# Gated mix of linear and softmax attention, one core: products of kv with the output weights in 16 tiles of 32x32, returned through DRAM

## The chip, the cores and the metric

The kernel runs on one core of a Trainium2 chip. The metric is the device time of one execution in microseconds, and the kernel before has a median of three runs. The engines are named as in the profile: PE is TensorE (PEld its weight loads), DVE is VectorE, ACT is ScalarE, POOL is GpSimd, SP is SyncE, which issues all DMAs here.

## The reference

Two attention blocks over the same x (1 x 2048 x 1024, fp32, 32 heads of 32) are mixed by a gate per token. B is softmax attention. A is linear attention: its kv is one 32x32 matrix a head, and its output goes through `wo`.

```python
x = A_x
g = _sigmoid((x * gate_w).sum(-1, keepdims=True))
# A: q, k, v = x @ wqkv, 32 heads
phi = lambda t: jnp.where(t > 0, t + 1, jnp.exp(t)) + 1e-6
pq, pk = phi(q), phi(k)
kv = einsum("bhsd,bhse->bhde", pk, v)
z = einsum("bhsd->bhd", pk)
num = einsum("bhqd,bhde->bhqe", pq, kv)
den = einsum("bhqd,bhd->bhq", pq, z)[..., None] + 1e-6
a = merge_heads(num / den) @ A_wo
# B
p = softmax(einsum("bhqd,bhkd->bhqk", q, k) * Dh ** -0.5)
b = merge_heads(einsum("bhqk,bhkd->bhqd", p, v)) @ B_wo
return g * a + (1 - g) * b
```

Since kv is the same for all tokens, the kernel does not form `num`: it multiplies each head's kv into that head's 32 rows of `A_wo` once, and the turned queries pq / den then go through the product.

## The kernel before, in words

All products of x and of the outputs with weights are fp32 in three products of a high and a low part (`three`, L148 to L150: high x high, high x low, low x high, each 128x128 by 512 columns). A part comes from a cast on ACT and a subtraction on DVE or POOL (`split`, L254 and L255). The main stage is one stream of PE instructions, made of several that a planner interleaves:

- `heads_`: for each of 32 heads, 64 score products (L902), each followed by an exponential on ACT (L906); in three groups of 5, 5 and 6 key blocks a head, the products with v (L994). A block is four products, each on a tile of 128x32 of the array, all into bank 4. The sums over keys are added on POOL (L951) and, for the last 512 columns, on DVE (L960). `finish` (L805) sums over partitions at the end of a head, just ahead of a group of the next head, and four reciprocals (L812) and a multiplication (L815) on DVE follow.
- `maxima`: the same 64 scores a head, transposed, two heads ahead (L752), each reduced on DVE (L757); `rows` (L762, L768) turns the maxima into two extra rows of the queries.
- `linear`: the chunks "v", "kv" (four), "q" (two) and "o" (two), each with 16 tiles of tokens and eight blocks k of the contraction. x tiles come from DRAM by `load_xp` (L479), two units ahead, for "o" the turned queries `oA_d`. Chunk "kv" accumulates kv of its eight heads in `keys` (L505, added on DVE in L514); "q" computes phi, divides (L660 to L674), and `queries` turns the tiles (L566) and stores them (L573); "o" writes its result to `ra_d` (L687, L688).

While the last token tile of a chunk runs, `split_w` replaces the eight weight blocks for the next chunk one by one, each block k after its last use. For "o" it is a product: the raw `a_wo` block (loaded by `load_w`, L262) is multiplied by `kvb`, a tile with the kv of four heads on the diagonal of 128x128 and zeros elsewhere (memset L635, copies L518), and the result is cast (L457) and subtracted (L458) into the weight tile:

```python
b = take()
end = lin_pe(4.0, free[b])
nc.tensor.matmul(pb, kvb[:, k, :], raw, start=True, stop=True)       # L455
```

That is sixteen products, eight ahead of each of the two "o" chunks; both operands are plain fp32, which runs as two passes.

Order: the instruction order on every engine is written out by the planner (`tc.manual_schedule`). It keeps an estimated end time for each engine (`T`, `use`), hands out the six PSUM banks of `RING` (`take`, `give`), defers DVE's work (`defer`, `fill`) and always advances the stream that is furthest behind its goal. The linear stream's pace in "kv" and "o" is

```python
cost = {"kv": NT * (D // HC) * (pace + 1) + 2 * (D // HC), "q": NQC * NT * (pace + 2),
        "o": NQC * (NT * pace + 4 * NK)}
rates["kv"] = rates["o"] = (cost["kv"] + cost["o"] - RESERVE) / (steps - cost["q"] / RATE_Q)
```

with pace 24, 2048 steps, RATE_Q 2.6 and RESERVE 56. After the last head, `output` multiplies B's output with `B_wo` and adds the two.

Of the kernel before, what the change touches and what calls it, by code (L numbers as in the profile page):

```python
# [45 lines left out]
def kernel(  # L46
# [32 lines left out]
    def f32(ap):  # L79
        return ap.bitcast(F32)  # L80
# [9 lines left out]

    xs = [[dram.tile([P, NK, P], F32, name=f"xs{p}_{t}") for t in range(NT)] for p in range(2)]
# [4 lines left out]
    v_d = [dram.tile([P, NT, C], F32, name=f"v{c}") for c in range(NQC)]  # L96
    ra_d = [dram.tile([P, D], F32, name=f"ra{t}") for t in range(NT)]
# [7 lines left out]
    kvb = sb.tile([P, NK, P], F32, name="kvb")  # L105
# [260 lines left out]
    kv_flat = kvb.rearrange("p k c -> p (k c)")  # L366

    def gate():
        for t in range(NT):
            for i in range(2):  # L370
                xn, junk = kv_flat[:, :HD], kv_flat[:, HD:]
# [62 lines left out]

    def load_w(kind, c, k, n):
        if kind == "v":
            raw = load_cols(b_wqkv, vcols(c), k, n)
        elif kind == "kv":
            raw = load_cols(a_wqkv, [(D + c * HC, HC), (2 * D + c * HC, HC)], k, n)
        else:  # L440
            raw = load_cols(a_wqkv if kind == "q" else a_wo, [(c * C, C)], k, n)
        return raw, T["pe"] + 4.0

    def split_w(kind, c, k, raw, at, eng):

        hi, lo = wpart(k, 0), wpart(k, 1)
        w_left[k].clear()
        if kind == "o":
            yield from keys_alone(len(units))
            need(k_left)  # L450
            yield lambda: both(bank_at(), at)
            b = take()
            pb = bank[b]
            end = lin_pe(4.0, free[b])
            nc.tensor.matmul(pb, kvb[:, k, :], raw, start=True, stop=True)  # L455
            end = use("act", 0.5, end)
            nc.scalar.copy(hi, pb)  # L457
            item = defer(lambda _: nc.vector.tensor_sub(lo, pb, f32(hi)), end)  # L458
# [32 lines left out]
    kv_acc = mid[8][:, :NK * DH].rearrange("p (k d) -> p k d", d=DH)  # L491

    def keys(n, c, t, pk, va, todo):
# [3 lines left out]
        def products(b, at):  # L497
# [9 lines left out]
            acc = kv_acc[:, c * GC:(c + 1) * GC, :]  # L507

            def total(_):
                part = pb.rearrange("p (k d) -> p k d", d=DH)  # L510
                if t == 0:
                    nc.vector.tensor_copy(acc, part)
                else:
                    nc.vector.tensor_add(acc, part, acc)  # L514
                if t == NT - 1:
                    for r in range(4):
                        rows = slice(r * DH, (r + 1) * DH)
                        nc.gpsimd.tensor_copy(kvb[rows, c * GC:(c + 1) * GC, rows], acc[rows])  # L518
# [16 lines left out]
    def keys_alone(n):  # L535

        while kv_todo and kv_todo[0][0] <= n:
            yield lambda: both(kv_todo[0][1](), bank_at()) if kv_todo else 0.0
            if kv_todo and kv_todo[0][0] <= n:
                use("pe", AV_SWITCH, kv_todo[0][1]())  # L540
                keys_now(T["pe"])

# [37 lines left out]
    def linear():  # L580
# [4 lines left out]
        for n, (i, t) in enumerate(units):  # L585
# [14 lines left out]
            for k in range(NK):  # L600
# [15 lines left out]
                if k == NK - 1:  # L616
                    yield from extra
                if follow and t == NT - 2 and k < min(LEAD_W, NK):
                    coming_w.append(load_w(*follow, k, LEAD_W + 1))
                if follow and t == NT - 1:  # L620
                    yield from split_w(*follow, k, *coming_w.popleft(), nc.vector if kind == "v" else nc.gpsimd)
# [9 lines left out]
            elif kind == "kv":  # L631
                va = mid[7][:, (n % 2) * HC:(n % 2 + 1) * HC]
                yield from keys_alone(n - 2)
                if c == t == 0:
                    nc.gpsimd.memset(kvb, 0.0)  # L635
# [48 lines left out]
            else:  # L684
                res = mid[8 + n % 2]
# [182 lines left out]
    def heads_():  # L868
# [3 lines left out]
        raws[2:6] = [spare[:, i * C:(i + 1) * C] for i in range(4)]  # L872
        o_ring.append(spare)
# [57 lines left out]
    def attend(h, lacc):  # L931
# [50 lines left out]
        def av(t0, t1):  # L982
# [95 lines left out]
    def output():  # L1078
# [30 lines left out]
        for n in range(NT):  # L1109
# [12 lines left out]
            "o": NQC * (NT * pace + 4 * NK)}  # L1122
# [111 lines left out]
```

## Time and profile before

| | |
|---|---|
| median of 3 runs | 2903.78 us (2903.44 to 2906.72) |
| the profiled execution | 2902.3 us |
| its span, first to last instruction | 2900.5 us |
| granted TensorE clock, mean | 0.999 |
| DMA moved, mean rate | 364.88 MB, 126 GB/s |

How to read the rows: a group has the line, the engine, the operation, output <- inputs with partitions x elements, then the count, busy microseconds, the mean nanoseconds of one, and the engine's idle time ahead of them with what ended it. "128*32" behind a matmul is rows * columns of the array that it uses. In a timeline the first number is the start in microseconds from the start of the span, the second the duration from the first to the last end of the merged instructions; matmuls are pipelined, so one that lasts 0.39 us may follow another after 0.23. In a row of windows stand the stretch, its length, busy time and count of PE, PEld, DVE, ACT and POOL, the granted clock, the busy share of the DMA engines and GB/s.

### The profile page before, as it was taken

What the parts mean: (1) busy time and instruction counts of PE and PEld (TensorE: products, weight loads), DVE (VectorE), ACT (ScalarE), POOL (GpSimd) and SP (SyncE); (2) the same over time, 40 slices, a digit from 0 to 9 for tenths busy, and PEclk for the clock granted to TensorE, in tenths of its full rate; (3) what the DMA queues carried; (4) which work ended last, traced back from release to release, by engine and by line L of the source; (5) the groups of instructions that cost most, each with busy time, mean ns of one, the idle gap of its engine ahead of it and who ended that gap; (6) DMA issues with size and microseconds to landing.
All of it is one profiled execution on the core that took longest, in us unless ns stands there. A gap on an engine that the chain in (4) does not pass through costs nothing.

```text
span 2900.5 us, 43785 instructions
## 1 busy us (share of the span) xinstructions
PE 2888.7 (100%) x15840; PEld 2076.8 (72%) x15840; DVE 2057.6 (71%) x3451; ACT 1522.4 (52%) x2840; POOL 1775.7 (61%) x599
## 2 busy tenths in 40 slices
PE   9999999999999999999999999999999999999999
PEld 8888888766666666767667667676666666666787
DVE  3222114888888888888888888888887888886622
ACT  4111111466666667666766666666566666666410
POOL 0000001388898889888898896787769887786000
PEclk9999999999999999999999999999999999999999
DMA  6687333322343224222333334545443334323542
GB/s 196 211 268 236 120 124 102 115 88 89 90 125 98 90 89 119 93 88 91 117 90 95 100 117 139 157 151 160 138 151 104 105 107 130 100 88 120 197 154 78
DMA packets 273309, 364.88 MB, mean 126 GB/s; under 512 B 91146, under 2 KB 167434, under 8 KB 269962
## 3 DMA queue, kind: packets, MB, share of 16 engines
q1 hardware_dynamic: 273092, 362.07, 40.6%
q8 instruction: 125, 2.05, 0.3%
q14 instruction: 92, 0.75, 0.1%
HBM read 260.31 MB, written 100.40 MB: 124 GB/s over the span
## 4 chain that ended last, share of the span: by engine, by line
PE 97%; POOL 1%; DMA 1%; DVE 1%; issue 0%; ACT 0%; SPq 0%; POOLq 0%; ACTq 0%
PE bank L902 16%; PE bank L148 16%; PE bank L150 16%; PE bank L149 16%; PE bank L752 16%; PE bank L994 15%; PE bank L805 1%; POOL big L951 1%; PE bank L566 1%; PE bank L505 0%; DVE mx L757 0%; PE bank L455 0%; DMA mid<-in_a_wqkv 0%; POOL big L465 0%; DMA mid<-in_xT 0%
## 5 line engine op out<-in xcount | busy, mean ns | idle before, releaser
L951 POOL TENSOR_TENSOR big<-big,big 128x1536 f32<-128x1536 f32 (+1 forms) x434 | 1556.7, 3587 | 188.0 <-ACT big L906 165.5
L757 DVE TENSOR_REDUCE mx<-bank 128x1 f32<-128x512 f32 x2048 | 1312.9, 681 | 318.4 <-PE bank L752 314.5
L906 ACT ACTIVATE big<-bank 128x512 f32<-128x512 f32 x2048 | 1181.5, 601 | 525.6 <-PE bank L902 455.9
L902 PE MATMUL bank<-big,big 128*128 128x512 f32 x2048 | 811.6, 398 | 1.1 <-DMA big<-ml 0.5
L752 PE MATMUL bank<-big,big 128*128 128x512 f32 x2048 | 807.9, 395 | 3.8 <-ACT big L906 2.5
L148 PE MATMUL bank<-big,big 128*128 128x512 f32 x2048 | 801.3, 391 | 1.5 <-ACT big L254 1.4
L150 PE MATMUL bank<-big,big 128*128 128x512 f32 x2048 | 799.2, 390 | 0.0
L149 PE MATMUL bank<-big,big 128*128 128x512 f32 x2048 | 799.1, 390 | 0.0
L902 PEld LDWEIGHTS bank<-big,big 128*128 128x128 f32 x2048 | 384.0, 188 | 164.5 <-issue 67.8
L994 PE MATMUL bank<-big,mid 128*32 128x512 f32 x4096 | 458.5, 593 | 0.0
L752 PEld LDWEIGHTS bank<-big,big 128*128 128x128 f32 x2048 | 384.8, 188 | 93.4 <-ACT big L906 6.2
L148 PEld LDWEIGHTS bank<-big,big 128*128 128x128 f32 x2048 | 384.8, 188 | 87.8 <-DVE mx L757 3.0
L149 PEld LDWEIGHTS bank<-big,big 128*128 128x128 f32 x2048 | 384.8, 188 | 80.1 <-issue 0.8
L150 PEld LDWEIGHTS bank<-big,big 128*128 128x128 f32 x2048 | 384.8, 188 | 79.7 <-DVE big L255 0.6
L707 POOL MEMSET big<- 32x2048 f32 x3 | 5.4, 1808 | 530.7 <-PE bank L149 459.6
L994 PEld LDWEIGHTS bank<-big,mid 128*32 128x32 f32 x4096 | 129.0, 110 | 262.4 <-issue 262.4
L960 DVE TENSOR_TENSOR bank<-bank,big 128x512 f32<-128x512 f32 (+1 forms) x434 | 280.8, 647 | 10.0 <-ACT big L906 8.0
L255 DVE TENSOR_TENSOR mid<-bank,mid 128x512 fp32r<-128x512 f32 x64 | 44.3, 692 | 264.6 <-ACT mid L254 264.6
L947 POOL TENSOR_TENSOR big<-big,big 128x1536 f32<-128x1536 f32 (+1 forms) x31 | 111.6, 3599 | 139.8 <-ACT big L906 139.8
L254 ACT CAST mid<-bank 128x512 fp32r<-128x512 f32 x64 | 37.6, 587 | 291.6 <-PE bank L150 262.5
L812 DVE RECIPROCAL bank<-bank 128x128 f32<-128x128 f32 x128 | 123.3, 963 | 3.3 <-PE bank L805 0.3
L255 DVE TENSOR_TENSOR big<-mid,big 128x512 fp32r<-128x512 f32 x96 | 64.2, 687 | 74.7 <-ACT big L254 74.5
(76 smaller groups left out, 998.0 us busy)
## 6 DMA issues: line engine op xcount, KB each, us to landing
big<-xs SPq DMA_DIRECT2D x192, 512.0 KB, 4.1
qk<-mid SPq DMA_DIRECT2D x128, 256.0 KB, 2.8
big<-oA SPq DMA_DIRECT2D x64, 512.0 KB, 4.1
big<-qk SPq DMA_DIRECT2D x96, 256.0 KB, 4.5
big<-qk SPq DMA_DIRECT2D x384, 64.0 KB, 2.0
xs<-big SPq DMA_DIRECT2D x64, 256.0 KB, 4.2
oA<-mid SPq DMA_DIRECT2D x64, 256.0 KB, 2.8
mid<-in_b_wqkv SPq DMA_DIRECT2D x48, 256.0 KB, 3.9
```

Of the source, the lines that this page charges most:

```text
L148: yield nc.tensor.matmul(ps, sh, mh_, start=(kt == 0), stop=False)
L149: yield nc.tensor.matmul(ps, sh, ml_, start=False, stop=False)
L150: yield nc.tensor.matmul(ps, sl, mh_, start=False, stop=(kt == NK - 1))
L752: nc.tensor.matmul(bank[b], q[:, t * P:(t + 1) * P], k[:, j * C:(j + 1) * C], start=True, stop=True)
L757: nc.vector.tensor_reduce(m[:, t, j:j + 1], bank[b], AX.X, ALU.max)
L812: nc.vector.reciprocal(pl[:, sl], pl[:, sl])
L902: nc.tensor.matmul(bank[b], k[:, t * P:(t + 1) * P], q[:, j * C:(j + 1) * C], start=True, stop=True)
L906: nc.scalar.activation(pr_t[i][:, j * C:(j + 1) * C], bank[b], AF.Exp, scale=SCALE)
L947: nc.gpsimd.tensor_add(lacc[:, :qp], pr(0)[:, :qp], pr(1)[:, :qp])
L951: nc.gpsimd.tensor_add(lacc[:, :qp], lacc[:, :qp], pr(t)[:, :qp])
L960: nc.vector.tensor_add(lacc[:, qp:] if t == NT - 1 else l_b[:, :n], l_b[:, :n], src)
L994: nc.tensor.matmul(av_b[j * DH:(j + 1) * DH, :], v[:, t, :], pr(t)[:, j * C:(j + 1) * C], start=(t == 0), stop=(t == NT - 1))
```

## The change

The products of kv with `a_wo` leave the change of weights. They are now done in four groups `mix()`, one for each half of the contraction (four blocks k) and each "o" chunk, each inside a group of products with v: sixteen products of 32 rows by 32 columns by 512, each head's kv with its own 32 rows of `a_wo`, on sixteen tiles of the array, into four banks of the ring (one a row group). `kvb` shrinks to the kv as accumulated (128 x 8 x 32), so the memset, the diagonal copies and the separate accumulator go. Each bank is cast on ACT and subtracted on DVE as before, and both parts are stored to DRAM (`wa_d`). At the last tile of the chunk before, `load_wa` loads the finished parts straight into the weight tiles. The raw `a_wo` blocks are loaded at tiles 2 and 8 of the first "q" chunk and of the first "o" chunk; tile 14 of these waits, in the planner, until the group is placed. A group is placed where the planner finds four of the six banks free, after at least two blocks of the group with v. The gate's scratch moves from `kvb` to a big tile, and the results of "o" use other tiles for their stores. The planner's cost of "o" loses its 4 NK a chunk.

```diff
-    kvb = sb.tile([P, NK, P], F32, name="kvb")
+    kvb = sb.tile([P, NK, DH], F32, name="kvb")
...
+    def load_wa(c, k):
+        for p in range(2):
+            nc.sync.dma_start(f32(wpart(k, p)), wa_d[p][k // HK][c][k % HK])
+        w_ready[k] = T["pe"] + 5.0
...
     def split_w(kind, c, k, raw, at, eng):
         hi, lo = wpart(k, 0), wpart(k, 1)
-        w_left[k].clear()
-        if kind == "o":
-            yield from keys_alone(len(units))
-            need(k_left)
-            yield lambda: both(bank_at(), at)
-            b = take()
-            pb = bank[b]
-            end = lin_pe(4.0, free[b])
-            nc.tensor.matmul(pb, kvb[:, k, :], raw, start=True, stop=True)
-            end = use("act", 0.5, end)
-            nc.scalar.copy(hi, pb)
-            item = defer(lambda _: nc.vector.tensor_sub(lo, pb, f32(hi)), end)
-            give(b, 0.0, [item])
-            w_left[k].append(item)
-            return
...
-                if t == NT - 1:
-                    for r in range(4):
-                        rows = slice(r * DH, (r + 1) * DH)
-                        nc.gpsimd.tensor_copy(kvb[rows, c * GC:(c + 1) * GC, rows], acc[rows])
...
+    mix_todo = deque((a, c) for c in range(NQC) for a in range(NK // HK))
+    mix_hi, mix_lo = [], (mid[7], mid[10], mid[0], mid[1])
+
+    def load_mix():
+        a, c = mix_todo.popleft()
+        for i in range(HK):
+            nc.sync.dma_start(mix_hi[i], a_wo[(a * HK + i) * P:(a * HK + i + 1) * P, c * C:(c + 1) * C])
+        mix_here.append((a, c, T["pe"] + 8.0))
+
+    def mix_ready():
+        times = [ended(readers[b], free[b]) for b in RING if not held[b]]
+        return (mix_here and not kv_todo and ended(k_left, mix_here[0][2]) is not None
+                and ended(k_left, mix_here[0][2]) <= T["pe"]
+                and sum(at is not None and at <= T["pe"] for at in times) >= 4)
+
+    def mix():
+        a, c, _ = mix_here.pop()
+        need(k_left)
+        bs = [take() for _ in range(4)]
+        end = use("pe", AV + 0.2)
+        for r in range(4):
+            rows = slice(r * DH, (r + 1) * DH)
+            for i in range(HK):
+                nc.tensor.matmul(bank[bs[r]][i * DH:(i + 1) * DH, :], kvb[rows, a * HK + i, :],
+                                 mix_hi[i][rows, :], start=True, stop=True)
+        for r in range(4):
+            hi, lo, pb = f32r(mix_hi[r]), f32r(mix_lo[r]), bank[bs[r]]
+            at = use("act", 0.5, end)
+            nc.scalar.copy(hi, pb)
+
+            def low(_, r=r, hi=hi, lo=lo, pb=pb):
+                nc.vector.tensor_sub(lo, pb, f32(hi))
+                for p, src in enumerate((hi, lo)):
+                    nc.sync.dma_start(wa_d[p][a][c][:, r * DH:(r + 1) * DH, :], f32(src))
+                mixed.append((a, c))
+
+            give(bs[r], 0.0, [defer(low, at)])
...
+            if kind in ("q", "o") and c == 0 and t in (2, 8, NT - 2):
+                yield lambda: None if mix_here else 0.0
+                if t < NT - 2:
+                    load_mix()
...
+                if follow and follow[0] == "o":
+                    if t == NT - 1:
+                        w_left[k].clear()
+                        yield lambda: 0.0 if mixed.count((k // HK, follow[1])) == 4 else None
+                        load_wa(follow[1], k)
+                    continue
...
-                res = mid[8 + n % 2]
+                res = mid[(7, 10)[n % 2]]
...
+        mix_hi.extend(raws[2:6])
...
-            end = use("pe", AV * len(blocks_))
             for t in blocks_:
+                if mix_here:
+                    fill(T["pe"])
+                    if t - t0 > 1 and mix_ready():
+                        mix()
+                end = use("pe", AV)
                 for j in range(NJ):
                     nc.tensor.matmul(av_b[j * DH:(j + 1) * DH, :], v[:, t, :], pr(t)[:, j * C:(j + 1) * C],
                                      start=(t == 0), stop=(t == NT - 1))
...
-            "o": NQC * (NT * pace + 4 * NK)}
+            "o": NQC * NT * pace}
```

More of the change, by code (lines that the diff above doesn't have):

```diff
@@ L96 @@
     v_d = [dram.tile([P, NT, C], F32, name=f"v{c}") for c in range(NQC)]
+    wa_d = [[[dram.tile([HK, P, C], F32, name=f"wa{p}_{a}_{c}") for c in range(NQC)] for a in range(NK // HK)]
+            for p in range(2)]
     ra_d = [dram.tile([P, D], F32, name=f"ra{t}") for t in range(NT)]
@@ L365 @@
     nc.sync.dma_start(zrep, bass.AP(tensor=gate_w.tensor, offset=gate_w.offset, ap=[[0, P], [1, D]]))
-    kv_flat = kvb.rearrange("p k c -> p (k c)")
+    gate_t = f32(big[LACC[1]])
     def gate():
@@ L440, in load_w @@
         else:
-            raw = load_cols(a_wqkv if kind == "q" else a_wo, [(c * C, C)], k, n)
+            raw = load_cols(a_wqkv, [(c * C, C)], k, n)
         return raw, T["pe"] + 4.0
@@ L490 @@
     kv_todo = deque()
-    kv_acc = mid[8][:, :NK * DH].rearrange("p (k d) -> p k d", d=DH)
     def keys(n, c, t, pk, va, todo):
@@ L506, in products @@
                                      start=True, stop=True)
-            acc = kv_acc[:, c * GC:(c + 1) * GC, :]
+            acc = kvb[:, c * GC:(c + 1) * GC, :]
             def total(_):
@@ L541, in keys_alone @@
                 keys_now(T["pe"])
+    mix_todo = deque((a, c) for c in range(NQC) for a in range(NK // HK))
+    mix_here = []
+    mixed = []
+    mix_hi, mix_lo = [], (mid[7], mid[10], mid[0], mid[1])
[17 more added lines that the diff above has]
+            for i in range(HK):
+                nc.tensor.matmul(bank[bs[r]][i * DH:(i + 1) * DH, :], kvb[rows, a * HK + i, :], mix_hi[i][rows, :],
+                                 start=True, stop=True)
+        for r in range(4):
[8 more added lines that the diff above has]
+            give(bs[r], 0.0, [defer(low, at)])
     z_end = [0.0, 0.0]
@@ L620, in linear @@
                 if follow and t == NT - 1:
-                    yield from split_w(*follow, k, *coming_w.popleft(), nc.vector if kind == "v" else nc.gpsimd)
+                    split_w(*follow, k, *coming_w.popleft(), nc.vector if kind == "v" else nc.gpsimd)
                     if k + LEAD_W < NK:
@@ L633, in linear @@
                 yield from keys_alone(n - 2)
-                if c == t == 0:
-                    nc.gpsimd.memset(kvb, 0.0)
                 nc.scalar.copy(va, ps[:, HC:])
```

2 lines of the change are left out of this document (1 added, 1 removed).

## The prediction

> **What bounds the kernel now.** I read the page first: busy times, chain.
>
> ```profile
> span 2900.5 us, 43785 instructions
> ...
> PE 2888.7 (100%) x15840; PEld 2076.8 (72%) x15840; DVE 2057.6 (71%) x3451; ACT 1522.4 (52%) x2840; POOL 1775.7 (61%) x599
> ...
> PE 97%; POOL 1%; DMA 1%; DVE 1%; issue 0%; ACT 0%; SPq 0%; POOLq 0%; ACTq 0%
> ```
>
> PE lies on 97% of the chain and is idle for 2900.5 - 2888.7 = 11.8 us in all. So the time is PE's work plus few waits: a microsecond of array time taken out is a microsecond of the kernel, unless a wait takes its place. Then the list of PE's waits, longest first (its first row), and the groups by shape that the change touches or leans on.
>
> ```profile
> PE bank L752 <- ACT big L906: 2.5, 2, 2.2
> ```
>
> ```profile
> L455 PE MATMUL bank<-big,kvb 128*128 128x512 f32 x22 | 11.6, 611 | 0.4 <-DVE big L458 0.4
> L455 PE MATMUL bank<-mid,kvb 128*128 128x512 f32 x10 | 5.2, 605 | 0.0
> L458 DVE TENSOR_TENSOR big<-bank,big 128x512 fp32r<-128x512 f32 x16 | 10.8, 678 | 0.0
> L457 ACT CAST big<-bank 128x512 fp32r<-128x512 f32 x16 | 9.4, 587 | 6.0 <-PE bank L455 6.0
> L994 PE MATMUL bank<-big,mid 128*32 128x512 f32 x4096 | 458.5, 593 | 0.0
> L994 PEld LDWEIGHTS bank<-big,mid 128*32 128x32 f32 x4096 | 129.0, 110 | 262.4 <-issue 262.4
> L518 POOL COPY kvb<-mid 32x64 f32<-32x64 f32 x16 | 3.7, 230 | 0.5
> ```
>
> The longest single wait of PE is 2.2 us. L455 shows 32 records: 16 products, each run as two passes. Their busy time, 16.8 us, overlaps their neighbours, so what one costs has to be read from starts, in the timeline of PE. First product, the dearest, and the last:
>
> ```profile
> 2132.65 0.39 PE L902 MATMUL bank<-big,big 128*128 128x512 f32 x1
> 2132.88 1.02 PE L455 MATMUL bank<-big,kvb 128*128 128x512 f32 x2
> 2133.33 0.80 PE L752 MATMUL bank<-big,big 128*128 128x512 f32 x1
> 2133.97 0.40 PE L902 MATMUL bank<-big,big 128*128 128x512 f32 x1
> ...
> 2136.74 0.40 PE L150 MATMUL bank<-big,big 128*128 128x512 f32 x1
> 2137.56 1.12 PE L455 MATMUL bank<-big,kvb 128*128 128x512 f32 x2 [0.43 <-DVE big L458]
> 2138.12 0.79 PE L752 MATMUL bank<-big,big 128*128 128x512 f32 x1
> 2138.76 0.40 PE L902 MATMUL bank<-big,big 128*128 128x512 f32 x1
> ...
> 2460.03 0.39 PE L902 MATMUL bank<-big,big 128*128 128x512 f32 x1
> 2460.26 1.02 PE L455 MATMUL bank<-mid,kvb 128*128 128x512 f32 x2
> 2460.72 0.80 PE L752 MATMUL bank<-big,big 128*128 128x512 f32 x1
> 2461.36 0.40 PE L902 MATMUL bank<-big,big 128*128 128x512 f32 x1
> ```
>
> An ordinary product starts 0.23 us after the one before it. From the start ahead of the first L455 to the second start behind it is 2133.97 - 2132.65 = 1.32 us; less two ordinary steps (0.46) L455 took 0.86 us from the chain. The last took 1.33 - 0.46 = 0.87, the dearest 2.02 - 0.46 = 1.56, since it stood behind the eviction of the product before it.
>
> **What goes.** All sixteen read this way give 15.1 us: fourteen between 0.86 and 1.01 (12.7 in all), the 1.56 above, and one behind a transpose that I put at 0.87. That is -15.1 us on the path. Also gone: the 16 POOL copies (0.23 us each) and a memset of the block-diagonal tile; POOL has 39% of the span free and no row of PE's waits names it, so nothing. The ACT casts and DVE subtractions stay sixteen each; they move.
>
> **What comes.** Four groups of sixteen 32x32 products, each put between blocks of L994's products with v, which use four 128x32 tiles. How tiles run side by side is seen at L994 and its weight loads:
>
> ```profile
> 2129.13 0.13 PEld L994 LDWEIGHTS bank<-big,mid 128*32 128x32 f32 x4 [0.30 <-issue]
> 2129.55 0.13 PEld L994 LDWEIGHTS bank<-big,mid 128*32 128x32 f32 x4 [0.30 <-issue]
> ...
> 2220.40 0.39 PE L752 MATMUL bank<-big,big 128*128 128x512 f32 x1
> 2220.72 1.06 PE L805 MATMUL bank<-big,ones 128*32 128x512 f32 x8
> 2221.60 4.48 PE L994 MATMUL bank<-big,mid 128*32 128x512 f32 x40
> 2226.01 0.50 PE L902 MATMUL bank<-big,big 128*128 128x512 f32 x1
> 2226.35 0.40 PE L148 MATMUL bank<-big,big 128*128 128x512 f32 x1
> ```
>
> Four weight loads of 110 ns fit into 0.13 us, so tiles start about (130 - 110) / 3 = 7 ns apart, and the next four come 0.43 us later: one pass takes 0.43 us for four tiles together, a block 0.86. If the four row groups run beside each other as the four column groups do here, sixteen tiles need 16 x 7 ns + 2 x 0.43 = 0.97 us. A change of tile shape: the entry step is 2220.72 - 2220.40 = 0.32 us against 0.23, +0.09; on the way out five blocks of 0.86 take 4.41 us (+0.11), and the step behind is 0.34 (+0.11). Entry and exit together are 0.31 us. A group inside the products with v changes shape twice more, so I charge one such pair: 0.97 + 0.31 = 1.28, four groups 5.1 us.
>
> No row of before has a row group of 32, so 0.97 is bounded from both sides. Below: nothing under the two passes, 0.86. Above: row groups one after another, 4 x 0.86 + 0.11 = 3.55. I take 0.97, by L994: column tiles already stream four different operands, and the sixteen add no more data per partition (each reads its own 32 partitions). The Trainium skill, "TensorEngine Tiling (Array Packing)", Key Properties, says that different tiles can load and multiply in parallel, sixteen of them in 32x32 form; no run shows it for rows. By it the four groups cost 5.1 us, by the four-at-a-time that the rows alone prove 4 x (3.55 + 0.31) = 15.4 us, and the change would be worth nothing.
>
> **Banks.** A group takes four of the six ring banks, and each comes back after a cast (0.59, ACT) and a subtraction (0.68, DVE): the first 1.27 us after the group, the fourth 0.59 + 4 x 0.68 = 3.3 us after it if DVE does nothing else. Cover: by the order of the changed program two to three blocks with v follow (1.7 to 2.6 us), then transposes or the linear product on its own bank, and the banks are asked for in the order in which they come free, with another product or two between. That fits without a wait. What can break it is DVE's own queue at a group:
>
> ```profile
> 2416.28 0.68 DVE L757 TENSOR_REDUCE mx<-bank 128x1 f32<-128x512 f32 x1
> 2416.88 3.96 DVE L812 RECIPROCAL bank<-bank 128x128 f32<-128x128 f32 x4
> 2420.87 0.69 DVE L815 TENSOR_TENSOR mid<-mid,bank 128x512 f32<-128x512 f32 x1
> 2422.14 1.38 DVE L757 TENSOR_REDUCE mx<-bank 128x1 f32<-128x512 f32 x2 [0.58 <-PE bank L752]
> ```
>
> In one of three places of a head four reciprocals (3.96 us) run there, and DVE is idle only 0.58 us behind them. In the changed order one of the four groups (the third, in the first output chunk) has these reciprocals ahead of its subtractions: its banks come about 4 us late, and I expect 1 us of waiting there; 0.2 at the others. Taken: 1.6 us in all. Bounds: 0, and 2.5 us a group (10) if DVE's backlog is not worked off.
>
> **Weights from DRAM.** Sixteen stores a chunk of 256 KB, and sixteen loads of 256 KB at the last tile of the chunk before, where eight loads of the raw weights were (these are now issued at tiles 2 and 8). DMA around the first such place, and the second:
>
> ```profile
> 2110.00:2140.00 30.00, 29.53 (x154) 19.39 (x153) 23.71 (x46) 19.11 (x38) 18.71 (x5) 1.00 0.79 218
> 2430.00:2460.00 30.00, 29.71 (x136) 18.32 (x135) 25.73 (x45) 19.91 (x38) 25.46 (x9) 1.00 0.26 85
> ```
>
> The first window moves 218 x 30 = 6.5 MB at a share of 0.79, so a full share is 218 / 0.79 = 276 GB/s. With 2.1 MB more it wants 8.6 MB, 31 us: just full. The second has room. Each load waits on SP for PE's last use of its weight tile; behind it on SP stand the stores of the turned queries, the next x tile and head's keys. By the changed order each pair of loads has about 9 to 15 us of PE work between its tile's release and its use, at 256 KB a load and 4 us to land. I put lateness at 0.3 us, bounds 0 and 3.
> The stores wait for casts and subtractions long before they are needed (tile 2 or 8 against tile 15): nothing. Planned pace: by its formula the output chunks' cost falls from 832 to 768 products and the rate from (1608 + 832 - 56) / 1728 = 1.38 to 1.34 per score step, so all orders from the first kv chunk on shift; PE's few waits (2.5 us at L752 the largest) may come or go: plus or minus 2.
>
> **Sum.** -15.1 + 5.1 + 1.6 + 0.3 = -8.1 us. The profiled execution took 2902.3 us (its span and 1.8 around it), so 2894.2; the median of the runs is 1.5 us above that execution, 2903.8, so I predict **2895.7 us**. What a measurement of this kernel tells from no change is about 0.2%, 5.8 us.
>
> **Rivals.**
> *Row groups take turns*, wholly (3.55 us a group) or because the second pass of one row group holds up the first of the next (then each row group adds one pass: 0.97 + 3 x 0.43 = 2.26). Groups then cost 4 x 2.57 = 10.3 or 15.4 us instead of 5.1: 2900.9 or 2906.0, no measurable change. For it: only four tiles at a time are seen. Against it: passes of four tiles interleave at L994 with no such hold. 0.14.
>
> *DVE becomes the bound behind each group* (the slower side). The place is the few microseconds behind each of the four groups. Price: fourth bank back at 3.3 us, plus 4.0 us of reciprocals or the query chain's operations that stand ahead, less 2.6 us of blocks: up to 4.7 us a group, 19 in all: 2903.8 - 10.0 + 19 = 2912.8. It cancels the gain from 2.5 us a group and is slower by more than 0.2% from 3.9. For it: DVE is busy 23.7 to 25.7 of 30 us in the windows above, and a head's maxima need it. Against it: it was idle 0.58 us after the reciprocals, and the linear product keeps PE for 24 steps on a single bank. The Trainium skill, "TensorEngine Tiling (Array Packing)", PSUM Bottleneck, warns of just this: tiling speeds up TensorE but not the emptying of PSUM, and the copies may become the bottleneck. The trace so far leaves slack at two of three places in a head, so I give it 0.10.
>
> *Weights late*: the DMA queues stay at the 218 GB/s they showed, 8.6 MB take 39.6 us, and PE waits 9.6 us once in place of 0.3: 2905.0. For it: share 0.79 already. Against: pairs are released one after another and used in the same order. 0.11, some of it slower.
>
> **Chances.** Forecast 0.65 (nearly all of it faster by over 0.2%), the three rivals 0.35, mostly no change. Faster 0.62, the same 0.24, slower 0.14. Range: downwards no bank waits, groups of 1.0 us and 2 us of luck: 2903.8 - 15.1 + 4.0 - 2 = 2890.7; upwards it takes in late weights and the milder turn-taking, 2905; beyond lie full turn-taking and DVE as the bound.
>
> **What would show it.** Right: in the changed profile sixteen-tile groups start within 0.11 us a pass, and a group lengthens its stretch of products with v by 1.2 to 1.4 us; no 128x128 product on the gathered kv; PE's span shorter by about 8; PE's waits on DVE behind groups under 1 us. Wrong: records of row groups that start 0.43 us or more apart (turns); PE waits on the new subtractions or on L757 of 2 us and more behind groups (DVE); PE waiting for the loads of the weights in the first tile of an output chunk (DMA).

## The result, and the profile after

The changed kernel takes 2922.81 us (median of 6 runs, 2921.77 to 2926.66) against 2904.2 us before in the same comparison (2903.44 to 2906.72): ratio 1.0065, interval 1.0052 to 1.0078. It is slower by 0.65%, where 2895.7 us was forecast with 2890.7 to 2905.0 as the range. The profiled execution took 2922.8 us, its span 2921.0. All times in this document leave out one execution of a kernel below (the loads in the 4 x 32 form), which took 4867.2 us at a granted clock of 0.56.

The page of the changed kernel, in the parts shown of before (lines of the kernel move: `three` is now L151 to L153, the scores L942, the maxima L791, the products with v L1038, the new 32x32 products L559, their cast L564, their subtraction L567, the stores of the parts L569; x tiles are loaded at L473, turned queries stored at L604):

```profile
span 2921.0 us, 44021 instructions
...
PE 2885.7 (99%) x15936; PEld 2073.3 (71%) x15936; DVE 2055.2 (70%) x3451; ACT 1522.7 (52%) x2840; POOL 1772.2 (61%) x582
...
PE 95%; DMA 2%; DVE 1%; ACT 0%; SPq 0%; issue 0%; ACTq 0%
```

PE's idle time was 11.8 us and is now 2921.0 - 2885.7 = 35.3. The list of PE's waits names it:

```profile
PE bank L151 <- DMA big<-xs: 21.2, 2, 15.1
...
PE bank L942 <- DVE mid L854: 0.2, 1, 0.2
```

Two waits for x tiles, 21.2 us together, of a kind that the list of before does not have. In the timeline of PE they stand behind the first and the second group of 32x32 products, both in the first q chunk:

```profile
1827.72 2.78 PE L1038 MATMUL bank<-big,mid 128*32 128x512 f32 x24
1830.43 1.16 PE L559 MATMUL bank<-big,kvb 32*32 32x512 f32 x32
1831.52 1.92 PE L1038 MATMUL bank<-big,mid 128*32 128x512 f32 x16
...
1859.86 0.76 PE L151 MATMUL bank<-big,big 128*128 128x512 f32 x1 [6.04 <-DMA big<-xs]
...
1904.58 0.76 PE L151 MATMUL bank<-big,big 128*128 128x512 f32 x1 [15.13 <-DMA big<-xs]
```

The group itself is as cheap as hoped. What delays the x tile is seen on SP, in the timeline of its DMA issues behind that group:

```profile
1815.73 0.80 SPq L473 DMA_DIRECT2D big<-xs  x2
...
1825.27 0.81 SPq L473 DMA_DIRECT2D big<-xs  x2
...
1832.35 0.61 SPq L569 DMA_DIRECT2D wa<-big  x1
...
1834.97 0.56 SPq L569 DMA_DIRECT2D wa<-mid  x1
1835.64 2.62 SPq L569 DMA_DIRECT2D wa<-big  x1
...
1843.43 2.46 SPq L569 DMA_DIRECT2D wa<-mid  x1
1845.99 2.94 SPq L604 DMA_DIRECT2D oA<-mid  x2
1849.02 2.58 SPq L762 DMA_DIRECT2D big<-qk  x3
1851.71 2.73 SPq L473 DMA_DIRECT2D big<-xs  x2
```

The second column runs from the start of the first issue in the row to the end of the last; in a row of one it is the time that SP spends on that issue. Four stores go out at 0.5 to 0.8 us each; from the fifth on each takes about 2.5 us, near the 2.9 us that 256 KB need at the 89 GB/s of the first window below, and everything behind them on SP waits: turned queries, keys of a head, and the next x tile, issued at 1851.71, 19 us after the first store and 26 after the x tile before it; the two x tiles ahead of the stores are 10 us apart. The same happens behind the second group, whose x tile goes out at 1897.94. The windows of these stretches (length, busy time and count of PE, PEld, DVE, ACT, POOL, granted clock, DMA share, GB/s):

```profile
1834.00:1845.00 11.00, 11.00 (x52) 9.08 (x51) 9.65 (x18) 7.47 (x14) 7.00 (x2) 1.00 0.26 89
...
1858.50:1865.30 6.80, 5.44 (x12) 3.92 (x13) 3.10 (x6) 3.27 (x6) 4.00 (x1) 0.50 0.94 297
1892.60:1909.70 17.10, 5.12 (x14) 4.20 (x15) 1.99 (x4) 1.19 (x2) 2.44 (x1) 0.50 0.75 243
```

While SP stands still, the DMA engines are busy to 0.26 and move 89 GB/s: a quarter of them, though stores are queued. And once PE has waited, the granted clock is 0.50 for 6.8 and 17.1 us; PE's work in these, 5.44 + 5.12 us, would have taken half of that, so the slow clock costs some 5.3 us beside the waits.

The account against the span of before (2900.5): -15.1 for the sixteen 128x128 products as in the prediction, +7.0 for the four groups (below), +21.2 for the x tiles, +5.3 for the clock, and +3.1 for PE's other waits (all rows of the list but that for x tiles: 10.4 us against 7.3): +21.5, where +20.5 is measured. The 1.0 between them is not explained.

### The profile page after: what moved, and what is told of

Read it like the earlier page. It is cut to its first block, busy times and chain, and to the rows that moved or that the text cites. A ratio compares the mean times of both kernels' runs of the same rounds, so it can differ in the third digit from the quotient of the medians.

```text
span 2921.0 us, 44021 instructions
## 1 busy us (share of the span) xinstructions
PE 2885.7 (99%) x15936; PEld 2073.3 (71%) x15936; DVE 2055.2 (70%) x3451; ACT 1522.7 (52%) x2840; POOL 1772.2 (61%) x582
## 4 chain that ended last, share of the span: by engine, by line
PE 95%; DMA 2%; DVE 1%; ACT 0%; SPq 0%; issue 0%; ACTq 0%
PE bank L942 16%; PE bank L791 16%; PE bank L151 16%; PE bank L153 15%; PE bank L152 15%; PE bank L1038 15%; PE bank L844 1%; DMA big<-xs 0%; PE bank L597 0%; DMA wa<-mid 0%; PE bank L498 0%; DMA big<-oA 0%; DVE big L1004 0%; DMA mid<-in_a_wqkv 0%; DMA big<-in_a_wo 0%; DVE mx L796 0%
## 5 line engine op out<-in xcount | busy, mean ns | idle before, releaser
L151 PE MATMUL bank<-big,big 128*128 128x512 f32 x2048 | 802.5, 392 | 25.1 <-DMA big<-xs 21.2
L942 PE MATMUL bank<-big,big 128*128 128x512 f32 x2048 | 810.7, 397 | 1.8 <-ACT big L946 1.7
L791 PE MATMUL bank<-big,big 128*128 128x512 f32 x2048 | 803.7, 393 | 2.8 <-ACT mid L316 2.6
L153 PE MATMUL bank<-big,big 128*128 128x512 f32 x2048 | 800.5, 391 | 0.4 <-DVE big L258 0.4
L942 PEld LDWEIGHTS bank<-big,big 128*128 128x128 f32 x2048 | 384.8, 188 | 159.0 <-issue 62.0
L151 PEld LDWEIGHTS bank<-big,big 128*128 128x128 f32 x2048 | 385.4, 188 | 115.2 <-issue 18.9
L1038 PE MATMUL bank<-big,mid 128*32 128x512 f32 x4096 | 459.2, 593 | 0.0
L791 PEld LDWEIGHTS bank<-big,big 128*128 128x128 f32 x2048 | 385.6, 188 | 86.6 <-ACT big L946 3.7
L153 PEld LDWEIGHTS bank<-big,big 128*128 128x128 f32 x2048 | 385.2, 188 | 82.8 <-DVE big L258 1.3
L1038 PEld LDWEIGHTS bank<-big,mid 128*32 128x32 f32 x4096 | 127.7, 110 | 263.7 <-issue 263.7
```

Of the source, the lines that this page charges most:

```text
L151: yield nc.tensor.matmul(ps, sh, mh_, start=(kt == 0), stop=False)
L153: yield nc.tensor.matmul(ps, sl, mh_, start=False, stop=(kt == NK - 1))
L791: nc.tensor.matmul(bank[b], q[:, t * P:(t + 1) * P], k[:, j * C:(j + 1) * C], start=True, stop=True)
L942: nc.tensor.matmul(bank[b], k[:, t * P:(t + 1) * P], q[:, j * C:(j + 1) * C], start=True, stop=True)
L1038: nc.tensor.matmul(av_b[j * DH:(j + 1) * DH, :], v[:, t, :], pr(t)[:, j * C:(j + 1) * C], start=(t == 0), stop=(t == NT - 1))
```

## The experiments

The theory: **the stores of finished parts, 4 x 32 x 512 in form, run on a quarter of the DMA engines, take 2.5 us each, and hold SP up ahead of x tiles that the q chunk needs every 10 us.** The rivals: it is the extra traffic in itself, whatever its form; it is the loads; or it is the groups on PE.

**Stores alone, in two forms.** To the kernel before are added sixteen stores of 256 KB of a tile that is at hand, in one place of the q chunk (for t = 6 the range is empty, so all go out at tile 9). Nothing else changes. The second kernel has the same bytes in the form 128 x 512.

```diff
+            if kind == "q" and c == 0 and t in (6, 9):
+                for i in range(8 if t == 6 else 0, 16 if t == 9 else 8):
+                    nc.sync.dma_start(wx_d[i // 4][:, (i % 4) * DH:(i % 4 + 1) * DH, :], zrep[:, :C])   # 4 x 32 x 512
+                    nc.sync.dma_start(wx_d[i // 4][i % 4], zrep[:, :C])                                 # or 128 x 512
```

> The kernel before, with two bursts of eight stores of 256 KB added at the start of tiles 6 and 9 of the first q chunk, from a tile that does not change to DRAM that nobody reads, in the form 4 x 32 x 512 of the change. Theory (the form puts each store on four of the sixteen DMA engines, so that it takes 2.5 us, SP stands still behind them and the x tiles come late): 8 to 25 us longer than before, with PE waiting for the x tile from DRAM one tile or two behind each burst. Rival (the waits come from the groups of sixteen tiles, their banks or the new order of work, not from the stores): within 2 us of before.

> The same bursts of the same bytes in the kernel before, each store as 128 rows of 512 in one block of DRAM. Theory (form): all sixteen engines, about 1 us a store, within 3 us of before. Rival (it is the bytes, or sixteen more transfers ahead of the x tiles on SP, whatever the form): as long as the kernel with the 4 x 32 form.

Measured: 2932.26 us, ratio 1.0099 (1.0084 to 1.0114), for the first; 2903.8, ratio 1.0001 (0.9991 to 1.001), for the second. The timeline of SP in the form 4 x 32 x 512:

```profile
1843.53 37.48 SPq L597 DMA_DIRECT2D wx<-zrep  x16
```

A window inside it:

```profile
1847.00:1855.00 8.00, 8.00 (x59) 4.35 (x52) 5.17 (x11) 2.86 (x6) 4.15 (x2) 1.00 0.26 89
```

The wait that follows, in ACT's timeline and in the list of PE's waits:

```profile
1892.61 0.59 ACT L569 CAST mid<-bank 128x512 fp32r<-128x512 f32 x1 [27.13 <-DMA oA<-mid]
```

```profile
PE bank L906 <- ACT big L910: 26.6, 2, 26.2
```

SP and such a window in the form 128 x 512:

```profile
1843.16 11.85 SPq L597 DMA_DIRECT2D wx<-zrep  x16
```

```profile
1844.00:1854.00 10.00, 10.00 (x67) 5.62 (x66) 6.96 (x13) 4.72 (x9) 6.11 (x2) 1.00 1.03 356
```

Equal bytes, equal place: 37.5 us of SP against 11.9, 89 GB/s against 356, a DMA share of 0.26 against 1.03. So the form is what costs, and 4 MB of traffic as such cost nothing here. The Trainium skill, "DMA: Bandwidth & Descriptors", section "Why a DMA increments its semaphore by 16 and not by 1", states the rule: a copy is spread over the largest number of engines up to 16 that divides the slowest dimension (other than 1) of both sides. That gives 4 engines for 4 x 32 x 512 and 16 for 128 x 512; the shares 0.26 and 1.03 agree. The first kernel is 28 us longer, above the 8 to 25 expected, and PE's wait comes by another way than was expected and than in the changed kernel: not the x tile but the store of the turned queries is late, ACT waits for it before it overwrites their tile, and the exponentials stand behind that on ACT. So this pair shows what the form costs, not that an x tile is what it must delay.

**No traffic of finished parts.** The groups, casts and subtractions stay; the stores and the loads of parts are left out, so the o chunks multiply by what stands in the weight tiles.

```diff
     def load_wa(c, k):
-        for p in range(2):
-            nc.sync.dma_start(f32(wpart(k, p)), wa_d[p][k // HK][c][k % HK])
-        w_ready[k] = T["pe"] + 5.0
+        w_ready[k] = 0.0
...
-                for p, src in enumerate((hi, lo)):
-                    nc.sync.dma_start(wa_d[p][a][c][:, r * DH:(r + 1) * DH, :], f32(src))
```

> The changed kernel without the stores of the finished weights and without their loads (the weight tiles keep what they held, so the A half of the output is left out of account). Theory: the waits for x tiles of 21 us and the slow clock behind them go, and what is left is the exchange of 16 products (15.1 us) for four groups (6.9 us): 2894 to 2898. Rival (new order or banks cost the time): stays above 2910.

Measured: 2895.22 us, ratio 0.9972 (0.9963 to 0.9981), no wait for an x tile. What the forecast missed therefore lies in the traffic. That the time is its 2895.7 within 0.5 is in part chance, since two of the four groups come ahead of their raw blocks here. The fourth group in PE's timeline:

```profile
2318.66 3.64 PE L1034 MATMUL bank<-big,mid 128*32 128x512 f32 x32
...
2326.16 1.13 PE L557 MATMUL bank<-big,kvb 32*32 32x512 f32 x26 [0.73 <-DMA big<-in_a_wo]
2327.22 3.55 PE L1034 MATMUL bank<-big,mid 128*32 128x512 f32 x16
```

From start to start this is 8.56 us, less eight passes of 0.43 us 5.1 for the group. Read in this way the four cost 1.2, 2.9, 1.4 and 5.1 us, 10.6 in all where the forecast had 5.1; banks cost next to nothing where it had 1.6, the loads of parts (0.3) are left out, and single executions lie between 2892.1 and 2902.3 us.

**The loads in that form, the stores flat.** The other half of the traffic:

```diff
-            nc.sync.dma_start(f32(wpart(k, p)), wa_d[p][k // HK][c][k % HK])
+            nc.sync.dma_start(f32(wpart(k, p)), wa_d[p][k // HK][c][:, (k % HK) * DH:(k % HK + 1) * DH, :])
...
-                    nc.sync.dma_start(wa_d[p][a][c][:, r * DH:(r + 1) * DH, :], f32(src))
+                    nc.sync.dma_start(wa_d[p][a][c][r], f32(src))
```

> The slow form moved from the stores to the loads: each store is 128 rows in one block of DRAM, each load of a weight part gathers 4 x 32 x 512. Theory (form): the stores cost nothing, but sixteen loads at 2.5 us ahead of each output chunk take 40 us where some 15 to 25 us of PE work cover them: PE waits 10 us or more at the first tile of each output chunk, 2905 to 2935. Rival (only stores to DRAM are slow in this form): 2893 to 2899.

Measured: 2946.81 us (median of three), ratio 1.0145 (1.0128 to 1.0161), above the 2905 to 2935 expected. The DMAs of the tile of parts (SP's ns of one, least, median and most) and PE's waits:

```profile
L441 SPq DMA_DIRECT2D big<-wa x32: 504/2000/7891, 2156.7 to 2514.5; - x32
L569 SPq DMA_DIRECT2D wa<-big x16: 319/397/600, 1830.4 to 2357.4; - x16
```

```profile
PE bank L152 <- DMA big<-wa: 17.0, 11, 2.8
PE bank L151 <- DMA big<-wa: 13.7, 9, 5.5
```

The stores fall to 0.40 us of SP, the loads rise to 2.0, and PE waits for weights 30.7 us where it did not wait for them at all. The cost goes with the form, not with the direction.

**Each store cut into four of 32 x 512.** Same bytes, no outer dimension of four, four times the issues; the second kernel also lets the planner place groups later, after the raw blocks have landed.

```diff
-                    nc.sync.dma_start(wa_d[p][a][c][:, r * DH:(r + 1) * DH, :], f32(src))
+                    for i in range(HK):
+                        nc.sync.dma_start(wa_d[p][a][c][i, r * DH:(r + 1) * DH, :], f32(src)[i * DH:(i + 1) * DH, :])
...
-        mix_here.append((a, c, T["pe"] + 8.0))
+        mix_here.append((a, c, T["pe"] + 16.0))       # in the second kernel
```

> The changed kernel with each store cut into four of 32 rows x 512 (64 KB), same bytes to the same places. Theory (a store in the form 4 x 32 x 512 uses four DMA engines): cut stores use all sixteen, the x tiles come in time and the gain of 8 us shows: 2893 to 2899. Rival (SP's issue, not the engines: 32 issues a group at 0.33 to 0.45 us are 11 to 14 us ahead of the x tiles): PE still waits 3 to 10 us for x tiles, 2899 to 2910.

> As the one before, and the planner counts 16 us instead of 8 from the issue of the raw a_wo loads to their arrival, so that a group is placed later. In the changed kernel the fourth group took 3.15 us instead of 1.20, since its loads came late. Theory (the late loads are the planner's estimate): 1 to 2 us less than the kernel with cut stores alone. Rival (loads were late only since SP stood behind slow stores): no difference, within 1 us.

Measured: 2906.25 us, ratio 1.0008 (0.9999 to 1.0017), and 2907.96, ratio 1.0018 (1.0009 to 1.0028). The first kernel's DMAs of the parts and its largest wait:

```profile
L570 SPq DMA_DIRECT2D wa<-big x64: 302/422/1532, 1832.9 to 2355.0; - x64
```

```profile
PE bank L151 <- DMA big<-xs: 10.6, 2, 10.4
```

Most of the loss goes, and the first kernel can't be told from the one before; but the gain of 8 us does not show, and the rival's waits of 3 to 10 us for x tiles are there: a group's 32 issues of 0.42 us are still 13 us of SP in one burst ahead of an x tile. SP's issues set the pace now, with the DMA engines busy to 0.55 from 1836 to 1847. In the second kernel the groups are at 1.20 us each, yet the 1 to 2 us less that were expected do not come. The waits only move: 5.6 us behind exponentials and 4.6 behind the rows of maxima, with 2.7 for x tiles. So two things count: how long the engines need, and how long the burst stands on SP.

**Uncut stores from POOL's queue.** SP then issues none of them.

```diff
-                    nc.sync.dma_start(wa_d[p][a][c][:, r * DH:(r + 1) * DH, :], f32(src))
+                    nc.gpsimd.dma_start(wa_d[p][a][c][:, r * DH:(r + 1) * DH, :], f32(src))
```

> The changed kernel with the stores issued by POOL in the uncut form; SP's queue holds none of them. Theory (two parts: stores on four engines, and SP standing still behind them): without the standing still the x tiles are issued in time and lose at most some 2 us on the four shared engines: 2894 to 2900, if POOL's own issue does not hold up its sums. Rival (the four engines' backlog alone delays each x tile whoever issues): PE still waits 10 us or more, 2906 or longer.

Measured: 2917.88 us, ratio 1.0045 (1.0031 to 1.0059). The stores' rows, and PE's largest wait:

```profile
L569 POOL DMA_DIRECT2D wa<-big x16: 688/691/827, 1834.1 to 2356.9; - x16
```

```profile
PE bank L151 <- DMA big<-xs: 13.7, 2, 11.2
```

No store stands on SP any more, and x tiles are still late by 13.7 of 21.2 us: the rival's 2906 or longer comes, and the theory that it is SP's own stores alone falls. A window behind the first group, and SP's timeline around it:

```profile
1838.00:1842.00 4.00, 4.00 (x19) 3.29 (x18) 3.93 (x7) 3.21 (x6) 2.95 (x2) 1.00 0.74 115
```

```profile
1819.03 1.26 SPq L762 DMA_DIRECT2D big<-qk  x3
1826.73 0.81 SPq L473 DMA_DIRECT2D big<-xs  x2
...
1843.80 6.89 SPq L762 DMA_DIRECT2D big<-qk  x3
1850.80 2.04 SPq L473 DMA_DIRECT2D big<-xs  x2
```

Two things follow. The DMA engines are busy to 0.74, and all packets recorded in this window are of POOL's queue, so from this queue the stores do not keep to a quarter of them, and the rival's "four engines" is not what this kernel tests. And SP isn't free though it holds no store: three loads of keys take it 6.89 us in place of 1.26, and the next x tile goes out 24 us after the one before it, against 26 in the change.

**Stores held back.** Three kernels keep the uncut stores in a list and issue them behind the loads of x tiles: three at a time in every chunk; two, or one, in the q chunk alone (there with groups as in the later kernel above).

```diff
-                    nc.sync.dma_start(wa_d[p][a][c][:, r * DH:(r + 1) * DH, :], f32(src))
+                    held_back.append((wa_d[p][a][c][:, r * DH:(r + 1) * DH, :], f32(src)))
...
             if n + 2 < len(units):
                 load_xp(n + 2)
+            put_back(3)                               # in the others 2 or 1, and at once in the o chunk
```

> The changed kernel with the stores held back and issued three at a time behind each load of an x tile, in the same 4 x 32 form. Theory (four engines, 2.5 us a store, and x tiles queued behind eight of them): with at most 7.5 us of stores between two x tiles the waits shrink below 4 us: 2895 to 2903. Rival (any store in this form delays loads in flight on the same engines, order matters little): 2910 to 2923.

> The changed kernel, with the stores of the two groups in the q chunk (16 of 256 KB, same 4 x 32 x 512 form, same queue) held in a list and issued two behind each load of an x tile, instead of eight at once ahead of it; the o chunk's stores go out at once as in the change. The raw blocks are loaded at tiles 1 and 9 of q instead of 2 and 8, and the planner expects them after 16 instead of 8 us. Theory (the time goes where a burst of stores stands on SP ahead of an x tile that is needed within 10 us): two stores are 5 us of the four engines' time per unit of 10 us, so no x tile is late; PE's waits on x tiles fall from 21.2 to under 2 us, the half clock behind them goes, and the array time saved shows: 2894 to 2898 us, ratio 0.997 to 0.998, under both kernels. Rival (stores in this form delay whatever shares their engines, wherever they stand): x tiles and turned queries stay late by some us, PE waits 5 us or more, 2900 to 2915 us.

> As the kernel with two stores behind each x tile, but one behind each, what is left going out together ahead of the next load of raw blocks and at tile 14. Theory: at one store a unit (2.5 us of 10) there is still less in front of an x tile, but seven or eight units hold the eight stores, so nothing is left in a burst: 2894 to 2898 us, the same as with two within 0.1%. Rival (stores delay what shares their engines, in proportion to their share): half the loss of the kernel with two, so clearly faster than that one by 2 us or more.

Measured: 2960.12 us, ratio 1.0192 (1.0175 to 1.0209); 2928.68, ratio 1.0079 (1.0062 to 1.0096); 2929.83, ratio 1.0089 (1.0074 to 1.0104). The theory's expectation failed in all three, and none came out as its rival had it: the first lies above 2923, the second above 2915, and the third is not faster than the second by 2 us or more but like it. (In the first, some stores go out in the o chunk after their tile has been used again, so part of the weights differs.) The wait for x tiles is gone in each, and others came: most in the first, where PE waits 35.0 us behind copies of o results. With two behind each x tile, one store in SP's timeline, SP's ns of one store of turned queries (least, median, most), PE's waits and ACT's:

```profile
1801.84 0.51 SPq L541 DMA_DIRECT2D wa<-big  x1
```

```profile
L611 SPq DMA_DIRECT2D oA<-mid x64: 319/338/762, 1773.4 to 2204.4; - x64
```

```profile
PE bank L951 <- ACT big L955: 11.3, 2, 8.8
```

```profile
ACT mid L606 <- DMA oA<-mid: 20.3, 3, 9.8
ACT mid L735 <- DMA wa<-mid: 7.7, 2, 4.2
```

SP is quick in the q chunk now, yet the turned queries' stores that follow (L611) land late: ACT waits for them at L606 three times, up to 9.8 us, before it may overwrite their only tile, and the exponentials queue behind it. That is the wait of the first experiment again. From 1810 to 1812, during one of these waits, the DMA share is 0.27 at 103 GB/s, a quarter of the engines again. L735, the copy of an o result, waits for a part that still lies in the tile it takes. So the rival "stores in this form delay whatever shares their engines" fits the mechanism, if not the size: taking them out of SP's way is not enough.

**Both halves mended.** Each store cut into four, held, and issued eight behind each x tile, in both chunks; the first o chunk's results go out from other tiles; groups as above. The second kernel loads the second group's raw blocks two tiles earlier and takes the result tiles later.

```diff
+                    for i in range(HK):
+                        held_back.append((wa_d[p][a][c][i, r * DH:(r + 1) * DH, :], f32(src)[i * DH:(i + 1) * DH]))
...
+            put_back(8)                               # behind load_xp(n + 2)
...
-                res = mid[(7, 10)[n % 2]]
+                res = mid[(7, 10)[n % 2]] if c else e
```

> The changed kernel, with both halves of the account mended: each store of a finished part is cut into four of 32 x 512 (64 KB), which run on all sixteen DMA engines, and they are held in a list and issued eight behind each load of an x tile, in the q and in the o chunk. The raw blocks are loaded at tiles 1 and 9 of q, with 16 instead of 8 us until the planner expects them, and the results of the first o chunk go out from two tiles that no part is stored from. Theory (two costs of the same form: the burst on SP ahead of x tiles, and the backlog of four engines behind which the turned queries' stores land late): eight pieces take 3.6 us of SP behind each x tile and leave no engine behind, so neither x tiles nor turned queries are late; PE's waits stay under 6 us in all, groups cost 1.2 us each, and the gain shows: 2893 to 2898 us, ratio 0.996 to 0.998, under both kernels. Rival (what was lost is the 4 MB of extra store traffic itself, however it is placed): waits of PE move elsewhere, 5 us or more of them remain ahead of exponentials, scores or x tiles, 2904 to 2915 us.

> As the kernel with held and split stores, with the second group's raw blocks loaded at tile 7 of q instead of 9, so that its stores are out before the raw weights of the next q chunk are loaded, and with the results of the first o chunk in the three tiles that the q chunk's phi used, each after its turned queries are read (before, the first results took such a tile too early and the last queries of q were lost). Theory (what was left, 4.3 us ahead of an exponential, came from turned queries that stood on SP behind pieces of parts and raw weights together): that wait goes, PE waits no more than before the change, and the whole of the array time shows: 2892 to 2896 us, ratio 0.996 to 0.997. Rival (extra traffic has its price wherever it stands): another wait of 3 us or more takes its place, 2899 to 2903 us.

Measured: 2900.73 us, ratio 0.9985 (0.9975 to 0.9994), for the first, above its 2893 to 2898: one wait of 4.3 us ahead of a score product is left. (In this kernel the first o results take a tile whose turned queries are still to be read, so the last queries of q are lost.) For the second 2893.09 us (5 runs, 2889.28 to 2893.86) against 2903.96, ratio 0.9957 (0.9943 to 0.9970), inside its 2892 to 2896. It beats the kernel before by 10.9 us and the change by 29.7. Its span, chain, largest wait, and one group:

```profile
span 2892.1 us, 44084 instructions
...
PE 98%; DMA 1%; DVE 1%; ACT 0%; issue 0%; SPq 0%; ACTq 0%
```

```profile
PE bank L151 <- ACT big L257: 3.0, 2, 1.9
```

```profile
1774.92 4.48 PE L1049 MATMUL bank<-big,mid 128*32 128x512 f32 x40
1779.33 1.16 PE L564 MATMUL bank<-big,kvb 32*32 32x512 f32 x32
1780.41 1.07 PE L1049 MATMUL bank<-big,mid 128*32 128x512 f32 x8
```

What is left of waits lies ahead of 700 us and behind 2500, in stages that the change does not touch. By terms: -15.1 + 4 x 1.2 - 0.3 for waits = -10.6; the medians differ by -10.9, the two profiled executions (2893.86 and 2902.3) by -8.4. The last kernel's has two stretches of 3.4 us at a granted clock of 0.50 where that of before has one, which is some 1.7 us of the 2.2 that are missing there.

## Why the prediction was wrong, by its own steps

- **What goes, -15.1**: not measured by itself, but with it the last kernel's sum closes within 0.3 us of the medians, and within 2.2 of the profiled executions (0.5 with the clock counted).
- **Groups, 4 x 1.28**: right in kind, 1.2 where nothing else is late. In the rows of the first group above, the start behind it less the first start of the products with v is 1831.52 - 1827.72 = 3.80 us, less six passes of four (0.43 each) 1.2. The group's row among the groups by shape, and the fourth group in PE's timeline:

```profile
L559 PE MATMUL bank<-big,kvb 32*32 32x512 f32 x128 | 6.5, 599 | 0.2 <-DMA big<-in_a_wo 0.2
```

```profile
2346.84 3.64 PE L1038 MATMUL bank<-big,mid 128*32 128x512 f32 x32
2350.41 1.16 PE L559 MATMUL bank<-big,kvb 32*32 32x512 f32 x4
2351.82 1.69 PE L559 MATMUL bank<-big,kvb 32*32 32x512 f32 x28 [0.24 <-DMA big<-in_a_wo]
2353.44 1.92 PE L1038 MATMUL bank<-big,mid 128*32 128x512 f32 x16
```

  One product is 0.60 us, so the last of the first group's 32 starts 1.16 - 0.60 = 0.56 us after its first; with a pass of 0.43 that is 0.99 us of array, where the prediction had 0.97 and the milder rival of turns 2.26. The row groups run beside each other, and what the Trainium skill's "TensorEngine Tiling (Array Packing)", Key Properties, says of sixteen tiles in parallel now has a trace that agrees. The second and third group cost 1.2 and 1.4, the fourth 2353.44 - 2346.84 less eight passes, 3.2, since it waits for its raw blocks inside: a term of 1.9 us that the prediction lacked, and that placing groups later removed.
- **Banks, 1.6**: too high. PE waits 0.2 us for DVE behind the groups in all. The rival "DVE becomes the bound" did not happen, and the warning in the Trainium skill's "TensorEngine Tiling (Array Packing)", PSUM Bottleneck, is not borne out here: 0.2 us.
- **Loads of weights, 0.3**: right; PE never waits for them in the changed kernel, so that rival is out as well.
- **Stores, "nothing"**: the step that failed. "The stores wait for casts and subtractions long before they are needed (tile 2 or 8 against tile 15)" asks only when their own data is due. It does not ask what one of them costs on SP and on the engines, nor who stands behind them; both were asked of the loads in the same paragraph. And it takes 256 KB as 256 KB, without a look at the form, for which the trace of before has no row and the Trainium skill's "DMA: Bandwidth & Descriptors" the rule cited above. Eight stores of 2.5 us are 20 us of those engines' work and 13.5 of SP's, on a queue from which an x tile is due every 10 us. Measured: 21.2 us of waits and 5.3 of half clock.
- **Pace, plus or minus 2**: 3.1 in the changed kernel, beyond its bound, and -0.3 in the last.

The slower side that was priced (2912.8 by DVE) had the wrong place; "the stores hold the queue" was due there. An estimate by the rule of the Trainium skill's "DMA: Bandwidth & Descriptors" cited above: a quarter of the prediction's 276 GB/s is 69 GB/s, at which 256 KB take 3.8 us and eight of them 30 us. Measured were 2.5, and 19 us from the first store to the x tile behind them.

What stays open: how the 21.2 us divide between SP's standstill and the engines' backlog. Cut into pieces the stores leave 10.6, held back uncut they leave none ahead of x tiles but more elsewhere, and from POOL's queue they leave 13.7, though there they run on more engines and still slow SP (three loads of keys take it 8.28 us behind the second group). None of these takes one of the two away and leaves all else as it was. In the last kernel cutting, spreading, later groups and other result tiles come together, so its gain isn't divided among them.

## What to carry to other kernels

When data goes through DRAM in a new form, cost the DMA by its form, not by its bytes: its outer dimension set here how many engines share it. For each burst name the queue, its length in time, and the shortest deadline among what stands behind it, on the queue and on the engines; a burst that isn't urgent is cut so that all engines take part, and spread behind the urgent loads. One of the two alone was not enough here: issued from another queue the burst still left 13.7 us of waits for x tiles, held back uncut it made others late.

## What the runs showed of the hardware

- A 256 KB store in the form 4 x 32 x 512 takes SP 2.5 us once four are under way, at a DMA share of 0.26; as 128 x 512 it takes 0.68 (median) at 1.03. A load of 256 KB in the 4 x 32 x 512 form takes SP 2.0 (median), in the flat form of the changed kernel 0.40.
- Issued from POOL's queue the same stores ran at a DMA share of 0.74 (1838 to 1842 us), and SP's own issues were slowed by them all the same: 6.89 us for three in place of 1.26.
- A wait of 6 us costs PE more than itself: the granted clock is 0.50 over 6.8 us around its end, and over 17.1 us around the wait of 15. The Trainium skill, "TensorE: Matmul & The Clock Gate", Part 1, states a half clock after an idle window of about 3.4 us and a return after a busy one; the stretches, two and five times 3.4 us, agree.
- Sixteen 32x32 tiles cost 1.2 us a group inside products on 128x32 tiles, two passes and both changes of shape included.
